# Row-wise reciprocal sums by a 32 by 32 turn and a trip through DRAM, packed remainder products, and a new order

## The chip, the cores and the metric

The kernel runs as one program on one core of a Trainium2 chip. The metric is device microseconds of one execution. The engines are TensorE (PE in the rows; its weight loads are PEld), VectorE (DVE), ScalarE (ACT), GpSimd (POOL) and SyncE (SP), which here only issues transfers.

## The reference

Three stages follow each other: attention with a threshold, a Fourier mixer with a channel MLP, and a token mixer with a gate.

```python
# 1. attention, B=4, H=8, S=576, D=64
scores = (q @ k.T) / sqrt(64)
scores = where(scores >= max(scores) - tau, scores, -1e9)
attn = exp(scores - max(scores)); attn = attn / (sum(attn) + 1e-9)
x = concat_heads(attn @ v)                      # [4, 576, 512]
# 2. Fourier mixing, then an MLP of 512 -> 2048 -> 512
u = x + real(fft(fft(x, axis=1), axis=2))
un = (u - mean(u)) / sqrt(var(u) + 1e-6)
x = u + relu(un @ w_ch1) @ w_ch2
# 3. token mixing with a gate, then a channel layer
theta = x @ w_theta
u = x + w_tok_r @ (x * cos(theta)) + w_tok_i @ (x * sin(theta))
out = u + relu(u @ w_ch)
```

## The kernel before, in words

All work is first described as named operations of one engine each, with a cost, a priority, what it comes after and which buffers it takes. A planner (`Plan.schedule`) then simulates the engines and writes the operations out in the order that it found. A long table (`SHIFT`) adds numbers to the priorities of single operations. On the chip every engine runs its own list strictly in that order and waits at semaphores.

**Attention.** The 32 heads go in 16 pairs (`pair`, p = 0 to 15). A pair has nine score tiles of 128 rows by 576 columns. For one tile TensorE makes the scores (`S`, lines 454 to 470), VectorE takes the negated row maximum (`evac`, line 478), ScalarE the exponential (`exp`, line 483), VectorE or GpSimd the bound (`bound`, lines 487 and 489), VectorE the masked product with the row sum in the same instruction (`mask`, line 494), TensorE transposes the result (`turn`, lines 501 and 541) and ScalarE copies it out of PSUM (`hi`, lines 510, 548, 550). When nine tiles are done, TensorE multiplies with the values into two banks `O` (`pv`, line 571, 256 and 320 columns), and VectorE multiplies each with the reciprocal sums into `xT` (`mu` and `mul`, line 576). The banks `O` are four; transposes, Fourier products and the reciprocal rows take theirs from the same four.

**The reciprocal sums.** The sums of a pair are nine columns of a [128, 9] tile, one per score tile: a sum sits in the partition of its row. The product at line 576 needs them along the free dimension, repeated over 64 partitions for each head. `norm_ops` does that: GpSimd adds 1e-9 (line 596), VectorE takes the reciprocal (599), GpSimd spreads eight columns to 512 (`Re`, 604), TensorE transposes four blocks (`Rt` part 0, line 611) and one more for the fifth column (part 1, line 613), and ScalarE copies both out of PSUM (`Rc`, lines 620 and 624).

**Fourier part.** `fft(b)` handles one of four batches, four pairs each. GpSimd and VectorE fold the tokens and channels, so that real transforms of quarter length are left, for an even and an odd kind. A few channels are left over: SyncE copies them into 16 rows of `exs` (line 721), ScalarE writes their rounded high part to `eys` (742) and GpSimd the low part into `exs` (746). The first transform is six products per kind and stage (`Xm`, line 775) and two more with `eys` and `exs` (`X`, line 785). The token rows beyond 128 of a kind go to `xrest`, high and low part in two slices, 31 or 33 rows each. The second transform (`Y`, line 814) uses three products for the main rows and three for `xrest`.

**Afterwards.** The channel MLP (lines 1102 to 1251; products at 1194 and 1214 to 1216) and the token mixer (1351 to 1551) are long runs of TensorE products. The MLP's normalised rows already go a way that the change uses too: VectorE turns 32 by 32 blocks (1150), SyncE stores them to DRAM in four transfers (990) and loads them back transposed (1158), and ScalarE reads them (1161).

**Transfers.** SyncE issues nearly all of them, in one list. Per pair that is a load of queries and keys (`raw`, line 304), the values (`vr`, 418), four copies into `L` (336, 337), eight into `H` and `X` (345, 346) and two corners (352). A transfer also waits for the one that used its completion semaphore eight transfers earlier.

**The start.** TensorE runs seven pairs of products on the identity (`warm`, line 393) while the first loads are under way; six pairs stand ahead of the first scores. The first scores (line 454) need a load of keys and one piece of queries that ScalarE scales (line 399, 384 columns).

Of the kernel before, what the change touches and what calls it, by code (L numbers as in the profile page):

```python
# [9 lines left out]
F32 = mybir.dt.float32  # L10
# [10 lines left out]
HS = S // 2  # L21
# [246 lines left out]
def attention_and_fft(pl, tc, ident, tb, pss, left, middle, right, qk, vv, cfk, cst, csr, u_d):  # L268
# [17 lines left out]
    ctr = lp.tile([128, 2, 640], F32R, name="ctr")  # L286
    xrest = lp.tile([128, 2, 258], F32R, name="xrest")
# [9 lines left out]
    def load_qk(p):  # L297
# [51 lines left out]
        def corner(e):  # L349
            for h, q in ((0, 512), (1, 0)):  # L350
# [5 lines left out]
        pl.op(("raw", p), *(("ACT", 620, -16.5) if first else ("SP", 2200, prio[0])), dma, [("ks", 4)] if first else (), [raw],  # L356
              delay=4500, fixed=p < 3)
# [11 lines left out]
              delay=4000)  # L369

# [4 lines left out]
    def load_first():  # L375
# [29 lines left out]
        pl.op("first pair", None, 0, -30, begin, (), [x])  # L405
        for i in range(WARM):
            after = [("warm", i - 1)] if i else []
            pl.op(("warm", i), "PE", 900 if i < 4 else 432, -40 + i, warm, after, [("O", "warm", i)])
# [6 lines left out]
    def load_v(p):  # L415
        def dma(e):
            VR[p] = new("vr", [128, 12, 64], f"vr{p}")
            e.dma_start(VR[p][:], vv[heads(p)])

        d, s = LOADS[7]  # L420
        pl.op(("vr", p), "SP", 1400, pr(9 * p - 9 + d, s) if p else -9, dma, [] if p > 1 else [("ks", 4)],
              [("vr", p)], delay=5000, fixed=p < 2)


    def pair(p):
# [3 lines left out]
        def tile_ops(idx):  # L429
# [61 lines left out]
            def mask(e):  # L491
                if "sums" not in st:
                    st["sums"] = mp.tile([128, 9], F32, tag="sums", bufs=3, name=f"sums{p}")
# [26 lines left out]
            pl.op(("S", k), "PE", 1060 if p == 0 else mm(6 if idx == 4 else 4, HS) + 25, pr(g - 1, 2), scores,  # L520
# [6 lines left out]
            pl.op(("mask", k), "DVE", 737, pr(g + 1, 7), mask, [("exp", k), ("bound", k)], (), [ps, P])  # L527
# [32 lines left out]
        def pv_ops(half, g):  # L560
# [12 lines left out]
            def mul(e):  # L573
                if p % 4 == 0 and not half:
# [7 lines left out]
            pl.op(("pv", k), "PE", 5 * TWO_PASS * n / 256 + 250, pr(g, 3), mms, deps + [("vr", p)], [O],  # L582
                  [("vr", p), ("pt5", p, 0), ("pt5", p, 1), (f"p0{half}", p), (f"p1{half}", p)])
            after = [("pv", k), ("Rc", p, half)] + ([("mu", p)] if half else []) + ([("mul", 4 * b)] if p % 4 else [])
            made = [xT] if p % 4 == 0 and not half else []
            pl.op(("mul" if half else "mu", p), "DVE", dve(n), pr(g + 1, 7.5), mul, after, made,
                  [O, ("R", p)] + ([] if made else [xT]))

        def norm_ops(g):
# [4 lines left out]
            def guard(e):  # L594
                st["rr"] = mp.tile([128, 9], F32, tag="rr", bufs=3, name=f"rr{p}")
                e.tensor_scalar(st["rr"][:], st["sums"][:], 1e-9, None, op0=ALU.add)
# [46 lines left out]
        norm_ops(g0 + 10)  # L643
# [6 lines left out]
    def fft(b):  # L650
# [82 lines left out]
        def extra_zero(e):  # L733
            if b == 0:
                e.memset(f32(xrest.rearrange("p a b->p (a b)")), 0.0)
# [8 lines left out]
        def extra_lo(e):  # L744
            x = exs[32:48, :289]
            e.tensor_sub(x.bitcast(F32R), x, f32(eys[32:48, :289]))
# [13 lines left out]
        def rows(kind, st):  # L760
            return slice(0, 128) if st < 2 else slice(64, 97) if kind == "e" else slice(0, 31)

        def first_ops(kind, st):
            loc = {}
            q = rows(kind, st)
            m = q.stop - q.start
            ki = "eo".index(kind)
            c0 = (0, size(kind) - 128, 128)[st]
# [10 lines left out]
            def part(i):  # L779
                return xrest[q, i] if st == 2 else X[kind][i][:, st]  # L780

            def more(e):
                ps = loc["ps"]
                for x, last in ((eys, False), (exs.bitcast(F32R), True)):
                    e.matmul(ps[:m, :258], x[:, c0:c0 + m], ctr[:, ki, :258], start=False, stop=last)
# [14 lines left out]
            pl.op(("Xm", k), "PE", mm(6, 258) + 80, pr(g, 3), mms, [("fl", (b, kind, a)) for a in range(2)] + ["tables"] +  # L800
                  gate(g), [O], [(f"{t}{kind}", b) for t in ("gh", "gl")])
            pl.op(("X", k), "PE", mm(2, 258), pr(g, 3), more, [("Xm", k), ("el", b)], (), [O, ("ex", b), ("ey", b)])
            pl.op(("Xh", k), "ACT", act(258), pr(g + 1, 4.2), hi, [("X", k)] + ([("Xh", (b, kind, 0))] if st else []),
# [1204 lines left out]
```

## Time and profile before

| | |
|---|---|
| time, median of 3 runs | 962.85 us (959.27 to 965.37) |
| the profiled execution | 962.4 us, span 960.5 us |
| TensorE busy | 937.9 us (98%) |
| VectorE busy | 626.9 us (65%) |
| ScalarE busy | 441.7 us (46%) |
| GpSimd busy | 301.9 us (31%) |

The span is from the first to the last instruction; the other 1.9 us of the profiled execution lie around it. A TensorE product's end is modelled, so a row of products that waits in between looks busier than it is; the distance from start to start of products that stand back to back is what one costs. The shares are means over two different halves: attention and most of the Fourier part until about 327 us, where four engines hand small tiles to each other, and the MLP and the mixer after it.

### The profile page before, as it was taken

The numbers are of one execution on the slowest core, as the hardware profiler recorded it, in microseconds if no ns is written. First come the engines' busy times: TensorE is split into PE (matmuls) and PEld (weight loads), VectorE is DVE, ScalarE is ACT, GpSimd is POOL, SyncE is SP. The second block draws the span as 40 slices with busy tenths as digits, with TensorE's granted clock in tenths as the row PEclk, the third lists the DMA queues.
The fourth block names the chain that finished last, engine by engine and source line by source line (L and its number), as shares of the span: only waits on it lengthen the run. The fifth ranks groups of instructions, "written<-read, shape, count | busy, mean of one in ns | idle before, by whom it ended". The sixth has DMA issues, their size and how long they took to land.

```text
span 960.5 us, 15977 instructions
## 1 busy us (share of the span) xinstructions
PE 937.9 (98%) x5746; PEld 807.1 (84%) x5746; DVE 626.9 (65%) x1225; ACT 441.7 (46%) x835; POOL 301.9 (31%) x468
## 2 busy tenths in 40 slices
PE   8899999999999999999999999999999999999998
PEld 6666788788778788888888888999988899999998
DVE  6777888898898889963553255232257475486832
ACT  6777877787777645530332132011143242253500
POOL 3466656657664643520232032000000021130100
PEclk9999999999999999999999999999999999999999
DMA  6897747765772478645893575241518612213011
GB/s 180 217 218 177 192 122 189 188 187 123 230 188 63 148 221 239 193 132 127 227 291 131 118 218 187 67 86 46 164 30 302 180 41 66 53 56 91 23 51 50
DMA packets 136623, 139.53 MB, mean 145 GB/s; under 512 B 77536, under 2 KB 98720, under 8 KB 136160
## 3 DMA queue, kind: packets, MB, share of 16 engines
q1 hardware_dynamic: 135520, 134.87, 50.9%
q0 software_dynamic: 720, 2.76, 1.1%
q8 instruction: 46, 0.75, 0.3%
q10 hardware_dynamic: 304, 0.87, 0.3%
q14 instruction: 33, 0.27, 0.1%
HBM read 77.34 MB, written 32.05 MB: 114 GB/s over the span
## 4 chain that ended last, share of the span: by engine, by line
PE 80%; DVE 5%; ACT 3%; DMA 2%; issue 1%; SPq 0%; DVEq 0%; POOL 0%
PE h L1194 20%; PE y L1474 12%; PE acc L1216 7%; PE acc L1214 7%; PE acc L1215 7%; PE f L1539 5%; PE th L1351 5%; PE O L571 5%; PE T L501 3%; PE ps L469 2%; PE ps L470 2%; DVE P L494 1%; DVE c L478 1%; ACT P L483 1%; PE ps L464 1%
## 5 line engine op out<-in xcount | busy, mean ns | idle before, releaser
L1194 PE MATMUL h<-uh,w 128*128 128x512 f32 (+1 forms) x640 | 197.5, 370 | 0.1
L1199 ACT ACTIVATE hh<-h 128x512 fp32r<-128x512 f32 (+1 forms) x80 | 44.4, 555 | 222.4 <-PE acc L1215 166.3
L1203 DVE SCALAR_TENSOR_TENSOR hl<-h,hh 128x512 fp32r<-128x512 f32 (+1 forms) x80 | 50.7, 634 | 135.9 <-ACT hh L1199 135.8
L1194 PEld LDWEIGHTS h<-uh,w 128*128 128x128 f32 x640 | 118.8, 188 | 17.3 <-DVE hl L1203 0.2
L494 DVE SCALAR_TENSOR_TENSOR P<-ps,c,P 128x576 f32<-128x576 f32 x144 | 115.1, 813 | 11.7 <-ACT P L483 9.2
L478 DVE TENSOR_REDUCE c<-ps 128x1 f32<-128x576 f32 x144 | 106.1, 750 | 21.1 <-PE ps L470 13.4
L1194 PE MATMUL h<-ul,w 128*128 128x512 f32 (+1 forms) x320 | 118.1, 369 | 0.0
L483 ACT ACTIVATE P<-ps,c 128x576 f32<-128x576 f32 x144 | 105.9, 749 | 22.5 <-DVE c L478 19.1
L1214 PE MATMUL acc<-w,hh 128*128 128x512 f32 x288 | 112.8, 392 | 0.0
L1216 PE MATMUL acc<-w,hl 128*128 128x512 f32 x288 | 112.6, 391 | 0.0
L1215 PE MATMUL acc<-w,hh 128*128 128x512 f32 x288 | 112.4, 390 | 0.0
L1474 PE MATMUL y<-w,z 128*128 128x288 f32 x768 | 106.9, 294 | 0.0
L1474 PEld LDWEIGHTS y<-w,z 128*128 128x128 f32 x768 | 104.0, 188 | 0.9
L501 PE MATMUL T<-ident,P 128*128 128x128 f32 x576 | 83.7, 275 | 4.6 <-DVE P L494 2.0
L510 ACT COPY pt<-T 128x512 f32<-128x512 f32 (+1 forms) x160 | 83.8, 555 | 9.1 <-PE T L501 8.2
L571 PE MATMUL O<-pt,vr 128*64 128x256 f32 (+1 forms) x640 | 84.7, 411 | 0.5 <-ACT R L624 0.5
L469 PE MATMUL ps<-H,L 128*128 128x288 f32 x240 | 75.7, 332 | 3.7 <-DVE P L494 3.0
L501 PEld LDWEIGHTS T<-ident,P 128*128 128x128 f32 x576 | 66.7, 140 | 11.7 <-ACT pt L510 4.5
L571 PEld LDWEIGHTS O<-pt,vr 128*64 128x64 f32 x640 | 43.1, 137 | 31.2 <-issue 3.9
L1194 PEld LDWEIGHTS h<-ul,w 128*128 128x128 f32 x320 | 60.1, 188 | 8.9
L470 PE MATMUL ps<-X,L 128*128 128x288 f32 x240 | 67.0, 295 | 0.0
L1216 PEld LDWEIGHTS acc<-w,hl 128*128 128x128 f32 x288 | 54.1, 188 | 11.8
(358 smaller groups left out, 1678.5 us busy)
## 6 DMA issues: line engine op xcount, KB each, us to landing
raw<-in_qk SPq DMA_DIRECT2D x14, 608.0 KB
vr<-in_vv SPq DMA_DIRECT2D x16, 384.0 KB
w<-w_d SPq DMA_DIRECT2D x6, 992.0 KB
H<-hs SPq DMA_DIRECT2D x30, 160.0 KB
X<-raw SPq DMA_DIRECT2D x30, 160.0 KB
X<-hs SPq DMA_DIRECT2D x30, 160.0 KB
H<-raw SPq DMA_DIRECT2D x30, 160.0 KB
mu<-u_d SPq DMA_DIRECT2D x18, 256.0 KB
```

The lines of the kernel that those rows point to most:

```text
L469: e.matmul(ps[:, half, :HS], L[:, qo:qo + 128], H[:, ko:ko + HS], start=(j == 0), stop=False)
L470: e.matmul(ps[:, half, :HS], L[:, qo:qo + 128], X[:, ko:ko + HS], start=False, stop=(j == n - 1))
L478: e.tensor_reduce(loc["c4"][:, 0:1], loc["ps"][:, :, :HS], axis=AXES.XY, op=ALU.max, negate=True)
L483: e.activation(halves(), loc["ps"][:, :, :HS], AF.Exp, bias=loc["c4"][:, 0:1], scale=1.0)
L494: e.scalar_tensor_tensor(halves(), loc["ps"][:, :, :HS], loc["c4"][:, 1:2], halves(), op0=ALU.is_ge, op1=ALU.mult, accum_out=st["sums"][:, ...
L501: e.transpose(T[:, kt * 128:(kt + 1) * 128], P[:, kt * 128:(kt + 1) * 128], ident[:])
L571: e.matmul(O[64 * h:64 * h + 64, :n], w, x, start=(kt == 0), stop=(kt == 4))
L1194: e.matmul(loc["ps"][:, :n], a, x[:, c, :n], start=(k == 0), stop=(k == 11))
L1214: e.matmul(a, hh[:, q], wh, start=(f == 0), stop=False)
L1215: e.matmul(a, hh[:, q], wl, start=False, stop=False)
L1216: e.matmul(a, hl[:, q], wh, start=False, stop=(f == NF - 1))
L1474: e.matmul(loc["ps"][:, half, :HS], z[:, cs], w, start=(n == 0 and m == 0), stop=(n == 8 and m == 2))
```

## The change: what it does

For pairs 4 to 15 `turned_ops` replaces `norm_ops`. The sums stand in one of three fixed [128, 32] tiles. VectorE takes the reciprocal and turns the tile in 32 by 32 blocks, so that each sum column becomes a row of 32 numbers in each of four partition groups. SyncE stores that to DRAM as 32 rows of 128 (16 KB), and then loads from there with a repeating pattern into 64 partitions per head: 576 numbers for the first head, 64 and 512 for the second (295 KB in all). No TensorE, ScalarE or GpSimd copy is left in it. Pairs 0 to 3 keep the old way.

In the Fourier part the low parts of the left-over channels go to other rows of `eys`, so that one product does the work of the two at line 785. `xrest` becomes one slice with the high part in some rows and the low part in others, so two products do the work of three at line 814. The even kind's third stage now comes after the odd kind's. `warm` falls from seven to four. The planner's costs of SyncE's loads change, the tables of constants load later, and the table of shifts has another last part, so that the whole order is new.

```diff
+TURNED_FROM = 4
-WARM = 7
+WARM = 4
...
-    ctr = lp.tile([128, 2, 640], F32R, name="ctr")
-    xrest = lp.tile([128, 2, 258], F32R, name="xrest")
+    ctr = lp.tile([128, 2, 898], F32R, name="ctr")
+    xrest = lp.tile([128, 258], F32R, name="xrest")
...
+    sums = [mp.tile([128, 32], F32, name=f"sums{i}") for i in range(3)]
...
-            after = [("pv", k), ("Rc", p, half)] + ([("mu", p)] if half else []) + ([("mul", 4 * b)] if p % 4 else [])
+            after = [("pv", k), ("Rc", p, half) if p < TURNED_FROM else ("rl", p)] + ([("mu", p)] if half else []) + ([("mul", 4 * b)] if p % 4 else [])
...
+        def turned_ops(g):
+            loc = {}
+            def guard(e):
+                e.tensor_scalar(sums[p % 3][:, :9], sums[p % 3][:, :9], 1e-9, None, op0=ALU.add)
+            def flip(e):
+                x = sums[p % 3]
+                e.reciprocal(x[:, :9], x[:, :9])
+                loc["t"] = mp.tile([128, 32], F32, tag="rt", bufs=2, name=f"rt{p}")
+                e.transpose(loc["t"][:], x[:])
+            def put(e):
+                e.dma_start(rr_d[p][:].rearrange("t (i j)->i t j", i=4), loc["t"][:])
+            def fetch(e):
+                R = st["R"] = new("R", [128, S], f"R{p}")
+                for h, q, t, o, n in ((0, 0, 0, 0, S), (1, 512, 4, 64, 64), (1, 0, 5, 0, 512)):
+                    e.dma_start(R[64 * h:64 * h + 64, q:q + n], bcast(rr_d[p][t:t + 1, o:o + 1], n, 64))
+            R = ("R", p)
+            pl.op(("guard", p), "POOL", 165, pr(g, 8.9), guard, [("mask", (p, i)) for i in range(9)])
+            pl.op(("inv", p), "DVE", 250, pr(g, 9), flip, [("guard", p)])
+            pl.op(("rs", p), "SP", 620, pr(g, 9.05), put, [("inv", p)], delay=2500)
+            pl.op(("rl", p), "SP", 1700, pr(g, 9.1), fetch, [("rs", p)], [R], delay=2500)
...
-        norm_ops(g0 + 10)
+        (norm_ops if p < TURNED_FROM else turned_ops)(g0 + 10)
...
-                for x, last in ((eys, False), (exs.bitcast(F32R), True)):
-                    e.matmul(ps[:m, :258], x[:, c0:c0 + m], ctr[:, ki, :258], start=False, stop=last)
+                e.matmul(ps[:m, :258], eys[:, c0:c0 + m], ctr[:, ki, 640:], start=False, stop=True)
...
-                mms += [(ctr[:, w, rest * 128:rest * 128 + 128], xrest[:, i]) for w, i in ((0, 0), (1, 0), (0, 1))]
+                mms += [(ctr[:, w, rest * 128:rest * 128 + 128], xrest[:]) for w in range(2)]
...
-FPLAN = {("e", 0): 13, ("e", 1): 15.1, ("e", 2): 17.2, ("o", 0): 19.3, ("o", 1): 21.4, ("o", 2): 23.5,
+FPLAN = {("e", 0): 13, ("e", 1): 15.1, ("e", 2): 23.5, ("o", 0): 17.2, ("o", 1): 19.3, ("o", 2): 21.4,
```

TensorE's list at the end of the last pair, before (T are transposes, R the reciprocal rows, xt the tokens, O the product with the values, of which ten follow):

```order
L541 MATMUL T515_1_4814<-ident_66,P15_5_4712 128x128
L541 MATMUL T515_1_4814<-ident_66,P15_7_4689 128x128
L501 MATMUL T15_6_4820<-ident_66,P15_5_4712 128x128 x4
L501 MATMUL T15_8_4826<-ident_66,P15_7_4689 128x128 x4
L611 MATMUL R15_0_4838<-ident_66,R15_4832 128x128 x4
L825 MATMUL xt2_0_1_4845<-ident_66,xT2_2753 128x128 x4
L571 MATMUL O15_0_4851<-pt15_00_4591,vr15_4371 64x256
```

The same place now, and behind the ten products of the first bank the products of the MLP's first tile `h0_0` up to the second bank:

```order
L505 MATMUL T15_6_4718<-ident_66,P15_5_4602 128x128 x4
L852 MATMUL xt2_0_1_4728<-ident_66,xT2_2770 128x128 x4
L545 MATMUL T515_1_4736<-ident_66,P15_5_4602 128x128
L545 MATMUL T515_1_4736<-ident_66,P15_7_4577 128x128
L575 MATMUL O15_0_4744<-pt15_00_4491,vr15_4263 64x256
```

```order
L1222 MATMUL h0_0_4764<-uh0_3512,w0_4715 128x512
L1222 MATMUL h0_0_4764<-ul0_3513,w0_4715 128x512
L1222 MATMUL h0_0_4764<-uh0_3512,w0_4715 128x512 x2
L1222 MATMUL h0_0_4764<-ul0_3513,w0_4715 128x512
L1222 MATMUL h0_0_4764<-uh0_3512,w0_4715 128x512 x2
L1222 MATMUL h0_0_4764<-ul0_3513,w0_4715 128x512
L1222 MATMUL h0_0_4764<-uh0_3512,w0_4715 128x512 x2
L1222 MATMUL h0_0_4764<-ul0_3513,w0_4715 128x512
L1222 MATMUL h0_0_4764<-uh0_3512,w0_4715 128x512
L575 MATMUL O15_1_4785<-pt15_01_4493,vr15_4263 64x320
```

The R rows are gone from TensorE, and the twelve products of `h0_0`, which stood behind both banks, now stand between them.

SyncE's list after pair 5's reciprocals, where the store of the turned sums and the loads of the rows are new, with the eight copies for pair 7 between them:

```order
L606 DMA rr_d5_122<-rt5_1734 4x32x32
L345 DMA H7_1755<-hs7_1525 64x640
L346 DMA X7_1756<-raw7_1308 64x640
L345 DMA X7_1756<-hs7_1525 64x640
L346 DMA H7_1755<-raw7_1308 64x640
L345 DMA H7_1755<-hs7_1525 64x640
L346 DMA X7_1756<-raw7_1308 64x640
L345 DMA X7_1756<-hs7_1525 64x640
L346 DMA H7_1755<-raw7_1308 64x640
L611 DMA R5_1819<-rr_d5_122 64x576
L611 DMA R5_1819<-rr_d5_122 64x64
L611 DMA R5_1819<-rr_d5_122 64x512
```

The list had only the eight copies there; four transfers per pair are added, and the first load waits until the store has landed.

VectorE's list from pair 15's reciprocal to its two products, now:

```order
L601 RECIPROCAL sums0_202<-sums0_202 128x9
L603 STREAM_TRANSPOSE rt15_4726<-sums0_202 128x32
L1091 TENSOR_TENSOR w0_4715<-v('w', 0)_3768,w0_4715 128x1024
L859 TENSOR_TENSOR u2_0_1_4759<-xt2_0_1_4728,sm2_0_4644 128x256
L861 TENSOR_TENSOR u2_0_1_4759<-xt2_0_1_4728,dm2_0_4613 128x4x63
L863 TENSOR_TENSOR u2_0_1_4759<-xt2_0_1_4728,dm2_0_4613 128x4
L1066 SCALAR_TENSOR_TENSOR raw('w', 2)_4659<-raw('w', 2)_4659 128x1024
L1070 SCALAR_TENSOR_TENSOR v('w', 2)_4756<-v('w', 2)_4756,raw('w', 2)_4659 128x1024
L580 TENSOR_TENSOR xT3_4039<-O15_0_4744,R15_4779 128x256
L580 TENSOR_TENSOR xT3_4039<-O15_1_4785,R15_4779 128x320
```

Six operations stand between the turn and the first product that needs the rows, where four stood between the reciprocal and it, and the two products now follow each other directly. In the other eleven turned pairs between 10 and 21 operations stand there.

## Rows read from the trace of the kernel before

**Rows 1.** The page's head and its first part.

```profile
span 960.5 us, 15977 instructions
...
PE 937.9 (98%) x5746; PEld 807.1 (84%) x5746; DVE 626.9 (65%) x1225; ACT 441.7 (46%) x835; POOL 301.9 (31%) x468
```

**Rows 2.** Busy time by window: busy us and count per engine, clock, DMA.

```profile
8.50:327.00 318.50, 303.88 (x2309) 243.88 (x2308) 271.45 (x632) 245.95 (x507) 188.55 (x363) 1.00 0.67 175
327.00:430.00 103.00, 102.34 (x506) 85.93 (x505) 90.82 (x117) 48.40 (x64) 47.74 (x35) 1.00 0.64 192
430.00:960.50 530.50, 524.68 (x2906) 470.81 (x2904) 263.91 (x471) 144.01 (x259) 63.39 (x58) 1.00 0.41 118
```

**Rows 3.** Timeline of TensorE, 104 to 117 us: start, length, operation.

```profile
105.93 0.66 PE L611 MATMUL R<-ident,R 128*128 128x128 f32 x4
106.34 0.38 PE L469 MATMUL ps<-H,L 128*128 128x288 f32 x1
...
107.49 0.27 PE L613 MATMUL R<-ident,rr 128*128 128x128 f32 x1
107.69 2.91 PE L571 MATMUL O<-pt,vr 128*64 128x320 f32 x20
...
113.44 0.37 PE L785 MATMUL Xe<-ctr,eys 128*128 128x258 f32 x1
113.65 0.29 PE L785 MATMUL Xe<-ctr,exs 128*128 128x258 f32 x1
113.77 0.60 PE L501 MATMUL T<-ident,P 128*128 128x128 f32 x4
```

**Rows 4.** Waits, 8.5 to 327 us: total us, times, longest.

```profile
DVE c L478 <- PE ps L470: 13.4, 19, 5.2
...
ACT R L624 <- PE R L613: 11.2, 8, 4.1
...
DVE P L494 <- ACT P L483: 9.2, 22, 2.3
...
ACT R L620 <- PE R L611: 7.1, 7, 2.1
...
DVE xT L576 <- PE O L571: 5.7, 6, 1.6
```

**Rows 5.** VectorE's groups, 8.5 to 327 us: busy, mean ns, idle before.

```profile
L494 DVE SCALAR_TENSOR_TENSOR P<-ps,c,P 128x576 f32<-128x576 f32 x144 | 115.1, 813 | 11.7 <-ACT P L483 9.2 <-POOL rr L596 0.3 <-POOL R L604 0.3
L478 DVE TENSOR_REDUCE c<-ps 128x1 f32<-128x576 f32 x144 | 106.1, 750 | 21.1 <-PE ps L470 13.4 <-PE ps L454 5.0 <-PE ps L464 2.1
...
L599 DVE RECIPROCAL rr<-rr 128x9 f32<-128x9 f32 x16 | 3.3, 206 | 1.1 <-POOL rr L596 1.1
```

**Rows 6.** ScalarE's copies of the reciprocal rows, whole span.

```profile
L620 ACT COPY R<-R 128x512 f32<-128x512 f32 x16 | 9.3, 584 | 7.4 <-PE R L611 7.1
...
L624 ACT COPY R<-R 64x64 f32<-64x64 f32 x32 | 6.6, 206 | 11.5 <-PE R L613 11.2
```

**Rows 7.** Timeline of SyncE, 629 to 651 us: the MLP's trip through DRAM.

```profile
630.50 1.94 SPq L990 DMA_DIRECT2D un_d<-un  x4
...
633.99 0.38 SPq L1158 DMA_DIRECT2D ul<-un_d  x1
```

**Rows 8.** Timeline of ScalarE, same stretch: the reader of those rows.

```profile
637.11 0.62 ACT L1161 CAST uh<-ul 128x512 fp32r<-128x512 f32 x1 [1.37 <-DMA ul<-un_d]
```

**Rows 9.** Timeline of SyncE, 158 to 170 us: one of eight copies.

```profile
164.87 0.60 SPq L345 DMA_DIRECT2D H<-hs  x1
```

**Rows 10.** Timeline of the start, all engines.

```profile
1.46 5.20 PEld L393 LDWEIGHTS warm<-ident 128*128 128x128 f32 x24 [1.46 <-POOL ident masks.py:199]
...
4.41 0.62 ACT L399 ACTIVATE x<-x,tb 64x384 f32<-64x384 f32 x1 [1.60 <-DMA x<-in_qk]
...
6.88 3.49 PE L454 MATMUL ps<-x 64*128 64x288 f32 x12
...
10.30 0.52 PEld L393 LDWEIGHTS warm<-ident 128*128 128x128 f32 x4 [0.39 <-issue]
```

More of the change, by code (lines that the diff above doesn't have):

```diff
@@ L265, in heads, with attention_and_fft @@
     return p + 3 - 2 * (p % 4)
-def attention_and_fft(pl, tc, ident, tb, pss, left, middle, right, qk, vv, cfk, cst, csr, u_d):
+def attention_and_fft(pl, tc, ident, tb, pss, left, middle, right, qk, vv, cfk, cst, csr, u_d, rr_d):
     nc = tc.nc
@@ L369, in load_qk @@
               delay=4000)
+    sums = [mp.tile([128, 32], F32, name=f"sums{i}") for i in range(3)]
+    for i in range(3):
+        pl.op(("sz", i), "POOL", 100, -25 + i, lambda e, i=i: e.memset(sums[i][:], 0.0))
     corners = [rp.tile([128, 128], F32R, name=f"corner{i}") for i in range(2)]
@@ L758, in gate, with rows @@
             return [("S", divmod(int(g), 9))] if b < B - 1 and g < 9 * NP else []
-        def rows(kind, st):
-            return slice(0, 128) if st < 2 else slice(64, 97) if kind == "e" else slice(0, 31)
+        def rows(kind, i):
+            return slice(64 * i, 64 * i + 33) if kind == "e" else slice(64 * i + 32, 64 * i + 64)
         def first_ops(kind, st):
             loc = {}
-            q = rows(kind, st)
-            m = q.stop - q.start
             ki = "eo".index(kind)
-            c0 = (0, size(kind) - 128, 128)[st]
+            m = 128 if st < 2 else (33, 32)[ki]
+            c0 = (0, size(kind) - 128, 128 - ki)[st]
             def mms(e):
@@ L799, in first_ops @@
             g = g0 + fp[kind, st]
-            pl.op(("Xm", k), "PE", mm(6, 258) + 80, pr(g, 3), mms, [("fl", (b, kind, a)) for a in range(2)] + ["tables"] +
+            pl.op(("Xm", k), "PE", mm(6, 258) + 80, pr(g, 3), mms, [("fl", (b, kind, a)) for a in range(2)] + ["tables", ("el", b)] + ([("Y", (b - 1, 1), kind)] if b else []) + [("X", (b, "o", 2))] * (st == 2 and not ki) +
                   gate(g), [O], [(f"{t}{kind}", b) for t in ("gh", "gl")])
-            pl.op(("X", k), "PE", mm(2, 258), pr(g, 3), more, [("Xm", k), ("el", b)], (), [O, ("ex", b), ("ey", b)])
-            pl.op(("Xh", k), "ACT", act(258), pr(g + 1, 4.2), hi, [("X", k)] + ([("Xh", (b, kind, 0))] if st else []),
+            pl.op(("X", k), "PE", mm(1, 258), pr(g, 3), more, [("Xm", k), ("el", b)], (), [O, ("ey", b)])
+            pl.op(("Xh", k), "ACT", act(258), pr(g + 1, 4.2), hi, [("X", k)] + ([("Xh", (b, kind, 0))] if st else []) + ([("Xl", (b, "o", 2))] if st == 2 and not ki else []),
                   [] if st else xs, [O] + (xs[:1] if st else []))
@@ L1823 @@
[L1823 to L1826 removed]
[6 rows of a table removed]
[17 rows of a table added]
+    (('Yp',), -36.02), (('a2',), 18.17), (('bound',), 18.79), (('bound', 0, 3), 123.45), (('bound', 12, 8), -65.39),
@@ L1863, in body @@
         x3_d = [dram.tile([128, 512], F32, name=f"x3_d{i}") for i in range(NT)]
+        rr_d = [dram.tile([32, 128], F32, name=f"rr_d{i}") for i in range(NP)]
         un_d = [dram.tile([512, 128], F32, name=f"un_d{i}") for i in range(NT)]
@@ L1938, in tables @@
     csr = np.zeros((128, 640))
-    for ki, r0, first in ((0, 64, (0, 0)), (1, 0, (1, 1))):
+    for ki, r0, first in ((0, 0, (0, 0)), (1, 33, (1, 1))):
         for par in range(2):
```

111 lines of the change are left out of this document (53 added, 58 removed), and 115 rows, old and new, of the table SHIFT.

## The prediction

> **What bounds the kernel now.** I read the page's head first: TensorE is busy 937.9 of 960.5 us [rows 1]. The view by window then shows that this is two cases [rows 2]. From 327 us on TensorE hardly rests (102.34 of 103 us, then 524.68 of 530.5), so there a product more or less counts with its full length. From 8.5 to 327 us the page still says 303.88 of 318.5, but ends of products are modelled, VectorE is busy 271.45 (85%) and ScalarE 245.95 (77%), and the list of waits has each waiting for another: VectorE 13.4 us for scores, 9.2 for exponentials, 5.7 for the products with the values [rows 4]. I take that stage as a pipeline of small tiles with TensorE as the densest engine and VectorE close behind. What is taken from TensorE there comes back in part.
>
> **What TensorE loses.** The cost of a product that does not wait is its distance to the next start [rows 3]. Four R transposes take 0.41 us (105.93 to 106.34), the lone one 0.20 (107.49 to 107.69): 0.61 a pair, times twelve pairs 7.3 us. A left-over product takes 0.12 us (113.65 to 113.77) and up to 0.21 with a change of tile before it (113.44 to 113.65). 24 go at line 785 (24 groups, one each) and 20 at line 814 (five groups in each of four batches, one each): 44 × 0.12 = 5.3 us, at most 9.2; the next products follow without a change, so I take 5.3. By the new order 31 of the 44 stand before the last pair's products and 13 behind. So TensorE loses 7.3 + 3.7 = 11.0 us in the stage and 1.6 behind it. The 1.6 counts whole. Of the 11.0 I count half, 5.5: nothing of it if VectorE sets the pace, all if TensorE does, and the rows put the two at 85% and at most 95%.
>
> **What ScalarE and GpSimd lose.** Per turned pair ScalarE loses a copy of 0.584 us and two of 0.206, 12.0 us in all [rows 6], and it no longer stands still in front of them (11.2 and 7.1 us for all sixteen pairs) [rows 4]. ScalarE at 77% hides that, except where an exponential was late; the 9.2 us of VectorE's waiting are the most there is. I count it inside the half above. GpSimd's spreading copy goes too; GpSimd has the most slack of the four [rows 2], so nothing.
>
> **What VectorE gains.** Twelve turns of 128 by 32. The trace has none of that size; the reciprocal of nine columns before it takes 0.206 us [rows 5], and a 576-column maximum 0.75. A turn lies nearest to the reciprocal: 0.2 × 12 = 2.4 us, bounds 0 and 9. VectorE has idle time of 15% next to it; half on the path, 1.2 us.
>
> **The new wait.** The product with the reciprocal rows stands in VectorE's strict list, so rows that come late stop VectorE and, behind it, every score tile. The same way through DRAM exists in the MLP: the last of four stores starts about 1.94 × 3/4 after 630.50, so near 631.95; the load that waits for it is issued at 633.99, 2.0 us later, and its reader, which waited for nothing else, starts at 637.11, 3.1 us after the issue [rows 7, 8]. The change's loads are three: the last starts about 0.9 us behind the first at 0.38 to 0.60 each [rows 7, 9]. With an idle list the way is 2.0 + 0.9 + 3.1 = 6.0 us.
>
> What VectorE has to do meanwhile follows from the new order and from durations. After pair 4's turn come four maxima at 0.75, four masked products at 0.81 and two small ones at about 0.21: 6.7 us of work, and at VectorE's 85% some 7.8 us of time. The same count gives 7.8 us for pair 10, 9.0 to 9.1 for 5, 8 and 14, 9.7 for 11, and 11.3 to 14.7 for 6, 7, 9, 12 and 13. Pair 15 has six operations of 3,580 columns together, at 0.813 us per 576 columns an estimate of 5.0 us, 5.9 in time. So eleven pairs have room for 6.0 us. Pair 5's loads stand behind eight copies of 0.6 us [rows 9]: 0.5 + 4.8 + 0.9 + 3.1 = 9.3 us, late by 0.3. Pair 15 has two weight loads of 512 KB between its store and its loads; at the stage's 175 GB/s [rows 2] these alone move for 6.0 us, so its rows are up to 5 us late. TensorE has `h0_0` and a bank of values for that time, of 2.75 and 2.8 us (twelve products of 512 columns, and ten of 320), so I count nothing for it, and nothing for the earlier `h0_0`. Lateness: 0.3 us.
>
> The four added transfers on SyncE take 4 × 0.6 = 2.4 us a pair, of about 20. Their neighbours wait 2 us more when a load stands directly behind its store, as for pairs 4 and 9. The loads for the next pairs are issued nearly a pair ahead, which hides that; without this cover each would cost its 2 us, 4 in all. That is in the range, not in the sum. The larger constant table and its later loads lie beside this work as well.
>
> The Trainium skill speaks against this step: "VectorE: DVE Perf Modes", section "Rules for kernel authors", sends a 128 by 128 transpose to TensorE, because VectorE turns only 32 by 32 blocks. The rows agree that TensorE's own price is small, 0.61 us a pair, and that the trip through DRAM is ten times as long; by that rule the exchange would lose, which is the rival "late rows" below. By the sum it does not, since the trip occupies neither engine.
>
> **The start.** 24 weight loads of `warm` take 5.20 us and the first scores start at 6.88, though the first piece that ScalarE scales was ready at 5.03 [rows 10]. Sixteen end near 5.0. That frees up to 1.7 us; since the next steps are VectorE's, I take 0.7.
>
> **Sum.** -5.5 - 1.6 - 0.7 + 1.2 + 0.3 = -6.3 us. The profiled execution took 962.4 us, 1.9 more than its span, and gives 956.1; the median of the runs is 0.45 us higher. I forecast **956.5 us**, 0.7% below 962.85. About 1% is what a measurement of this kernel can tell from no change: 953.2 and 972.5 us are its bounds.
>
> **The rivals.**
> - Half the relief arrives, as above: 956.5, own range 951 to 961. Chance 0.44.
> - *TensorE sets the pace of the stage.* For it: its busy share is the highest there. Against: it waits for VectorE and ScalarE too. Then 11.0 + 1.6 + 1.7 go, and the turn costs nothing: 962.85 - 14.3 = 948.5. Chance 0.24.
> - *VectorE sets it.* For it: 85% busy, with maxima and masked products that nothing shortens. Against: 28 us of waiting for TensorE and ScalarE. Only 1.6 + 0.7 go and the turns cost 2.4: 962.4, no gain. Chance 0.17.
> - *Late rows.* The trip through DRAM ends behind the bulk copies on the same queue in most pairs. For it: the queue's engines are 67% busy in the stage [rows 2], and only one trip in the trace is clean enough to read. Against: the 3.1 us above are for 256 KB, nearly the same bytes. With a trip of 11.5 us pairs 4 and 10 are late by 3.7 each, 5, 8 and 14 by 2.5, 11 by 1.8: 16.7 us, against 6.6 us of gains, 973: slower than before. It decides at a trip of about 9.8 us. Chance 0.10.
> - *A cold start.* In the trace the first 24 weight loads come 0.217 us apart and the four at 10.30 come 0.13 apart [rows 10]: the granted clock rose from its lower level (1.2 GHz) to 2.4 GHz in between, after TensorE had worked on `warm` without a break. With a third of that gone it may rise later. Pair 0's nine score groups at half the clock take about 1.9 us instead of 1.0, against 1.6 of VectorE's work, so some 3 us over nine: 959.5. Chance 0.05. The Trainium skill, "TensorE: Matmul & The Clock Gate", Part 1, says that throttled is the default and sustained activity releases it; the trace agrees in direction, and no run here has a shorter `warm`.
>
> That the change does not do what it says is excluded by the order: the R rows are gone in twelve pairs.
>
> **Range and chances.** 946 to 966 leaves out the lower edge of the second case and the late rows' upper half, under 2 in 10. Faster by over 1%: nearly all of the second case and a quarter of the first, 0.35. Slower by over 1%: over half of the late rows, 0.06. Within 1%: 0.59.
>
> **What would show it.** The last product of pair 15 with its rows (line 576; the end of the first long window, 327 us, was put there) moves to about 321 if the half is right, 315 if TensorE set the pace, and stays if VectorE did. VectorE's waits at line 580 for transfers of R: under 2 us without pair 15 if the trip is 6 to 8 us; over 10 if late rows decide. Twelve turns near 0.2 us. First scores near 5.2 us, and at the second clock level by about 8 us. From there to the end TensorE's busy share stays near 99%; new holes in the MLP, where the order is also new, would make the forecast too low.

## The result: 973.4 us, slower by 1.2%

The changed kernel takes 973.39 us (median of 4 runs, 972.58 to 976.79), the kernel before 962.0 beside it: ratio 1.0123, interval [1.0082, 1.0165]. The forecast was 956.5 us, range 946 to 966. The profiled execution is the longest of the four, 976.79 us with a span of 975.0.

The page's first part, and the windows cut where the last product of pair 15 ends (342.4 us now, 327 before), as in [rows 1, 2]:

```profile
span 975.0 us, 15763 instructions
...
PE 938.3 (96%) x5630; PEld 800.6 (82%) x5630; DVE 618.3 (63%) x1236; ACT 433.7 (44%) x805; POOL 286.6 (29%) x454
```

```profile
8.50:342.40 333.90, 305.83 (x2221) 239.55 (x2220) 271.76 (x637) 238.48 (x475) 178.37 (x352) 0.99 0.68 178
342.40:445.00 102.60, 98.96 (x474) 81.85 (x473) 84.94 (x115) 45.23 (x61) 49.02 (x30) 0.98 0.62 190
445.00:975.00 530.00, 526.60 (x2918) 473.35 (x2916) 260.07 (x478) 146.58 (x264) 57.03 (x57) 1.00 0.41 119
```

In a row of windows stand its bounds and length, then busy us and count of TensorE, its weight loads, VectorE, ScalarE and GpSimd, then the granted clock, the DMA share and GB/s. The first window has become 15.4 us longer; from its end to the span's end it is 632.6 us against 633.5. The whole loss lies in the attention stage. TensorE has 88 products fewer there and yet 28.1 us without work in place of 14.6. The waits of the stage (8 to 345 us), against [rows 4]:

```profile
ACT P L488 <- DVE c L483: 33.1, 31, 3.7
ACT pt L514 <- PE T L505: 20.8, 26, 2.7
DVE c L483 <- PE ps L475: 11.8, 25, 1.8
DVE P L498 <- ACT P L488: 11.4, 22, 2.1
...
DVE xT L580 <- DMA R<-rr_d: 10.5, 8, 3.9
DVE c L483 <- PE ps L459: 8.6, 8, 3.5
...
DVE u L859 <- DMA u_d<-u: 5.5, 2, 4.3
...
DVE bs L1135 <- DMA mu<-u_d: 2.3, 2, 1.9
```

and all of VectorE's waits for transfers before, in the same window:

```profile
DVE u_t L832 <- DMA u_d<-u: 2.2, 2, 1.9
...
DVE u L832 <- DMA u_d<-u: 1.8, 1, 1.8
```

VectorE's waits for transfers have grown from 4.0 to 18.3 us: those for the rows (line 580, 10.5 us) and for loads of `mu` (2.3) are new, and the wait for the store that frees the one buffer of `u` now has a stop of 4.3 us where the longest was 1.9. The other engines then wait for VectorE. Pair 5 shows the first, in the timelines of SyncE, VectorE and TensorE:

```profile
123.37 0.58 SPq L606 DMA_DIRECT2D rr_d<-rt  x1
124.05 0.48 SPq L345 DMA_DIRECT2D H<-hs  x1
...
129.35 0.59 SPq L346 DMA_DIRECT2D H<-raw  x1
129.99 2.00 SPq L611 DMA_DIRECT2D R<-rr_d  x3
```

```profile
130.89 0.76 DVE L483 TENSOR_REDUCE c<-ps 128x1 f32<-128x576 f32 x1 [1.17 <-PE ps L469]
135.53 0.42 DVE L580 TENSOR_TENSOR xT<-O,R 128x256 f32<-128x256 f32 x1 [3.88 <-DMA R<-rr_d]
```

```profile
131.44 1.15 PE L505 MATMUL T<-ident,P 128*128 128x128 f32 x8
136.01 0.66 PE L505 MATMUL T<-ident,P 128*128 128x128 f32 x4 [3.42 <-DVE xT L580]
```

The turn had ended at 122.1. The store, eight copies and three loads stand one behind the other; the rows are used 13.4 us after the turn, VectorE stands 3.88 us and TensorE 3.42. What follows has a price of its own: the granted clock falls to its lower level (1.2 GHz) for 3.4 us behind this stop of TensorE and behind that of 3.56 us for `u`, which ends at 259 us, as the windows show (mean clock third from the end). By an estimate, half of 3.4 us, each fall costs at most 1.7 us. A third, at 358.6 us, lies behind the stage.

```profile
136.70:140.10 3.40, 3.40 (x17) 3.38 (x16) 2.76 (x7) 2.73 (x6) 2.45 (x4) 0.50 0.27 96
259.60:263.00 3.40, 3.40 (x15) 1.60 (x16) 3.17 (x9) 2.43 (x4) 3.19 (x4) 0.50 0.74 206
```

### The profile page after: what moved, and what is told of

Its sections match the earlier page's. It is cut to its first block, busy times and chain, and to the rows that moved or that the text cites. A ratio compares the mean times of both kernels' runs of the same rounds, so it can differ in the third digit from the quotient of the medians.

```text
span 975.0 us, 15763 instructions
## 1 busy us (share of the span) xinstructions
PE 938.3 (96%) x5630; PEld 800.6 (82%) x5630; DVE 618.3 (63%) x1236; ACT 433.7 (44%) x805; POOL 286.6 (29%) x454
## 4 chain that ended last, share of the span: by engine, by line
PE 73%; DMA 9%; DVE 7%; ACT 4%; SPq 3%; issue 2%; POOL 1%; DVEq 0%; ACTq 0%; POOLq 0%
PE h L1222 20%; PE y L1502 12%; PE acc L1242 7%; PE acc L1244 7%; PE acc L1243 7%; PE f L1567 5%; PE th L1379 5%; PE O L575 3%; DVE c L483 2%; DMA R<-rr_d 2%; PE T L505 2%; DMA H<-hs 2%; DVE P L498 2%; PE ps L459 2%; ACT P L488 2%
## 5 line engine op out<-in xcount | busy, mean ns | idle before, releaser
L498 DVE SCALAR_TENSOR_TENSOR P<-ps,c,P 128x576 f32<-128x576 f32 x144 | 114.9, 813 | 13.5 <-ACT P L488 11.4
L505 PE MATMUL T<-ident,P 128*128 128x128 f32 x576 | 86.6, 280 | 14.7 <-DVE xT L580 4.3
L1411 POOL TENSOR_TENSOR tok<-tok 128x512 f32<-128x512 f32 x8 | 10.6, 1321 | 223.8 <-ACT tok L1401 123.0
```

Source lines behind the costliest of these rows:

```text
L498: e.scalar_tensor_tensor(halves(), loc["ps"][:, :, :HS], loc["c4"][:, 1:2], halves(), op0=ALU.is_ge, op1=ALU.mult, accum_out=st["sums"][:, ...
L505: e.transpose(T[:, kt * 128:(kt + 1) * 128], P[:, kt * 128:(kt + 1) * 128], ident[:])
```

## The experiments

Theory A: the transfers of the rows cost the time, since the rows come late. A2: not by their own lateness, but by what they do to the other transfers in SP's list. B: the cold start costs it. C: the new order of the work. Later A2w (SP's wait for the store), D (bytes on the DMA engines), L (SP's issue time) and P (packets) divide A2. "Ratio" is always to the kernel before on the same chip.

**Twelve identity products ahead of the scores, as before.**

```diff
-            for i in range(2):
...
+            warmed.append(0)
+            for i in range(6 if len(warmed) == WARM else 2):
```

> The changed kernel with four more products of the identity ahead of the first scores, 12 instead of 8, as the kernel before has; nothing else differs. Theory A (the rows of the sums come late and TensorE waits): the cold start is a small matter, its 4.7 us at the end of pair 0 have shrunk to 1.5 us by pair 2, so the time stays within 1.5 us of 973.4 us. Theory B (the cold start carries through): the full clock is granted near 8 us instead of 20.7 us, and the time falls by 4 to 5 us, to about 969 us.

Measured: 973.05 us, 1.014 [1.0112, 1.0169]. Of B's 4 to 5 us nothing shows, and the fastest of the four runs is 971.74: B falls. A gain or loss of a microsecond could not be told here.

**Rows not read, and no transfers at all.** The first edit; the second run also leaves out the store and the loads.

```diff
-                e.tensor_mul(xTs[b][:, j, a:a + n], loc["O"][:, :n], st["R"][:, a:a + n])
+                R = f32(cfs[:]).rearrange("p a b c d->p (a b c d)") if p >= TURNED_FROM else st["R"]
+                e.tensor_mul(xTs[b][:, j, a:a + n], loc["O"][:, :n], R[:, a:a + n])
```

> The changed kernel in which the products of pairs 4 to 15 with the reciprocal rows read a constant table in SBUF in place of the rows (the output is then not normalised for these pairs). The turns, the store and the three loads of every pair are still issued, and nobody waits for them. Theory A, in its direct form (VectorE's wait for the rows is the loss): the 10.5 us of waits at line 580 go, and the half-clock stretch behind the longest of them, so 961 to 965 us. Theory A2 (the loss is SP's list: four more issues per pair make SP's other transfers late): little goes, 968 to 973 us. Theory C (the new order of the work on the engines loses by itself): 970 us or more, and the next run shows no gain either.

> As the run whose products read a constant table, and the store and the three loads of each of the pairs 4 to 15 are not issued at all (the output of these pairs is not normalised); TensorE's relief and VectorE's turns stay. Theory A and theory A2: 956 to 961 us, since the transfers cause all of the loss but the cold start. They differ in how much of it the run before this one had already. Theory C: 970 us or more. My own prediction of 956.5 us assumed the transfers to cost 0.3 us, so this run also prices the relief without them: 956 us with half of it on the path, 950 us with all of it.

Measured: 968.86 us, 1.009 [1.0063, 1.0118], and 958.32 us, 0.9978 [0.9959, 0.9997]. Reading the rows costs some 4.5 us (973.4 - 968.9; the two ratios' intervals overlap, but each of the eight runs with readers, of the changed kernel and of the one with twelve products, is slower than each of the four without); having the transfers at all, read by nobody, 10.5 (968.9 - 958.3). Theory A in its direct form is the smaller part, A2 the larger, C is not needed for the loss.

**The short warm-up in the kernel before.** Two of its identity groups emit nothing.

```diff
...
+            warmed.append(0)
+            if len(warmed) in (5, 6):
+                return
```

> The kernel before with only 8 of its 12 products of the identity ahead of the first scores, all else as it was. Theory B (what starts cold stays late): full clock near 20 us, and 4 to 5 us more, 966 to 967 us. Theory A (the late start is made up within a few pairs, because VectorE or ScalarE sets the pace there): within 1.5 us of 962 us.

Measured: 961.95 us, 1.0027 [0.9999, 1.0056]. That is 2.6 us more [-0.1, 5.4]. The last masked product comes 5.0 us late in pair 0 and 2.7 in pair 15 of its profile. Between the two expectations, and small.

**The same transfers from other queues:** from ScalarE, from GpSimd (`nc.gpsimd`), and the loads alone from ScalarE.

```diff
-                e.dma_start(rr_d[p][:].rearrange("t (i j)->i t j", i=4), loc["t"][:])
+                nc.scalar.dma_start(rr_d[p][:].rearrange("t (i j)->i t j", i=4), loc["t"][:])
...
-                    e.dma_start(R[64 * h:64 * h + 64, q:q + n], bcast(rr_d[p][t:t + 1, o:o + 1], n, 64))
+                    nc.scalar.dma_start(R[64 * h:64 * h + 64, q:q + n], bcast(rr_d[p][t:t + 1, o:o + 1], n, 64))
```

> The changed kernel with the store and the three loads of the rows issued by ScalarE instead of SP, at the same places of the program. The run without the transfers took 958.3 us, the one in which they run unread 968.9 us. Theory A2 (what costs is their place in SP's list: the four issues and the wait for the store hold back SP's other transfers): SP's list is as without them, so 960 to 966 us, what is above 958 being ScalarE's own price for four issues and one wait per pair. Theory D (their bytes hold up the 16 DMA engines): no gain, 969 us or more.

> As the run with ScalarE, but GpSimd issues the store and the three loads. Theory A2: 960 to 966 us; GpSimd is busy 287 us of 975, less than ScalarE with 434 us, so not above the run with ScalarE. Theory D: 969 us or more.

> The changed kernel with the store of the rows on SP and only the three loads on ScalarE: SP is rid of three issues and of the wait for the store, ScalarE takes them. Theory A2w: SP's other transfers are on time, 965 to 970 us, what is above 958 being the rows' own lateness (4.5 us) and ScalarE's issues and waits. Theory D: 972 us or more.

Measured: 971.73 us, 1.0135 [1.0098, 1.0172]; 984.85 us, 1.026 [1.0229, 1.0291]; 983.84 us, 1.0233 [1.0206, 1.0261]. All three miss A2's numbers, but don't speak for D either: the issuing engine now stands still itself. From ScalarE, VectorE's waits for exponentials are 20.7 us (11.4 in the changed kernel) and the waits for the rows still 9.6. Those for the store of `u` are 1.8 us there (5.5 in the changed kernel) and none for `mu` is left, so SP's list is relieved as A2 has it, and the time is paid elsewhere. GpSimd stands 14.9 us for the store, with its small steps for VectorE behind it:

```profile
DVE P L498 <- ACT P L488: 20.7, 33, 2.0
DVE xT L580 <- DMA R<-rr_d: 9.6, 6, 5.1
...
DVE u L859 <- DMA u_d<-u: 1.8, 2, 1.2
```

```profile
POOL R L611 <- DMA rr_d<-rt: 14.9, 6, 4.7
```

**Sixteen bytes per transfer,** with the products reading the constant table; in the second run the loads read what the store wrote.

```diff
-                e.dma_start(rr_d[p][:].rearrange("t (i j)->i t j", i=4), loc["t"][:])
+                e.dma_start(rr_d[p][:1, :4], loc["t"][:1, :4])
...
-                    e.dma_start(R[64 * h:64 * h + 64, q:q + n], bcast(rr_d[p][t:t + 1, o:o + 1], n, 64))
+                    e.dma_start(R[64 * h:64 * h + 1, q:q + 4], bcast(cst[0:1, 0:1], 4, 1))
```

> As the run whose products read a constant table (pairs 4 to 15 are not normalised), SP still issues one store and three loads per pair, but each moves 16 bytes, and the loads take them from a constant in DRAM and so don't wait for the store. What is left of the transfers is four issues, some 2.4 us of SP's list per pair. Theory A2 by the issues: near the 968.9 us of the run with the full transfers unread, 965 to 969 us. Theory A2 by the wait for the store, or theory D (bytes): near the 958.3 us without transfers, 958 to 961 us.

> As the run with 16 bytes per transfer, but the three loads read what the store has just written, so that SP waits for it (pairs 4 to 15 are not normalised). The mirror of the run before: theory A2w: 967 to 969 us; theory D: 960 to 963 us.

Measured: 960.69 us, 1.0004 [0.9982, 1.0025], and 959.57 us, 0.9998 [0.9982, 1.0014]. Waiting for the store costs nothing that shows. So 8 us depend on what the transfers carry.

**Two loads in place of three,** with a source that walks over the two halves, then 64 repeats, then the columns.

```diff
-                for h, q, t, o, n in ((0, 0, 0, 0, S), (1, 512, 4, 64, 64), (1, 0, 5, 0, 512)):
-                    e.dma_start(R[64 * h:64 * h + 64, q:q + n], bcast(rr_d[p][t:t + 1, o:o + 1], n, 64))
+                for q, o, step, n in ((0, 0, 640, 512), (512, 512, 64, 64)):
+                    x = rr_d[p][:1, :1]
+                    src = bass.AP(tensor=x.tensor, offset=x.offset + o, ap=[[step, 2], [0, 64], [1, n]])
+                    e.dma_start(R[:, q:q + n], src)
```

> The changed kernel with two loads of the rows per pair instead of three, which move the same bytes: one for the first 512 queries of both halves, one for the other 64 of both. Theory A2 by the issues: one of the four issues goes, 0.6 us per pair, so about a quarter of the 10.5 us that the unread transfers cost, 970 to 971.5 us. Theory A2 by the wait for the store, or theory D: as the changed kernel, 973 us.

Measured: 1020.14 us, 1.0651 [1.0596, 1.0706], which no theory had. Waits of VectorE and, behind it, of TensorE's weight loads, 8 to 400 us:

```profile
DVE xT L580 <- DMA R<-rr_d: 56.0, 20, 5.9
PEld T L505 <- DVE xT L580: 28.0, 11, 5.6
```

The loads land later (more on this in the last section). It is a large dose of lateness: 56.0 - 10.5 = 45.5 us more of waiting at line 580, 3.8 us a pair, and 46.7 us more time. TensorE's weight loads stand 28.0 us of it with VectorE, and its clock has fallen often: the mean granted clock is 0.91 here between 100 and 400 us (third from the end), and 0.99 in the changed kernel between 100 and 345 us.

```profile
100.00:400.00 300.00, 249.08 (x1720) 202.32 (x1720) 211.30 (x495) 175.00 (x346) 132.47 (x265) 0.91 0.57 143
```

So the near equality of 45.5 and 46.7 is not a price of one for one: in the changed kernel, taking away 10.5 us of the same waiting gave back 4.5.

**Bytes, packets or SP's time.** Four variants with the rows unread, the full store, and the loads from a constant: with all bytes; with half the columns; with 64 different rows in place of one row 64 times; with 16 bytes in each of the 64 packets. The fifth is the kernel with 16-byte transfers of one packet, with seven loads instead of three.

```diff
...
+                    e.dma_start(R[64 * h:64 * h + 64, q:q + n], bcast(csr[0:1, 0:1], n, 64))
...
+                    e.dma_start(R[64 * h:64 * h + 64, q:q + n // 2], bcast(csr[0:1, 0:1], n // 2, 64))
...
+                    e.dma_start(R[64 * h:64 * h + 64, q:q + n], csr[64 * h:64 * h + 64, 0, :n])
...
+                    e.dma_start(R[64 * h:64 * h + 64, q:q + 4], bcast(csr[0:1, 0:1], 4, 64))
...
+                    for k in range(3 if q else 2):
+                        e.dma_start(R[64 * h + k:64 * h + k + 1, q:q + 4], bcast(cst[0:1, 0:1], 4, 1))
```

> As the run whose products read a constant table (pairs 4 to 15 are not normalised) with the full transfers, but the three loads of each pair take as many bytes from a constant in DRAM, and so don't wait for the store. Four issues with 16 bytes each took 960.7 us, with their full bytes and the wait for the store 968.9 us: 8.2 us lie between. Theory A2w (SP stands at the first load until the store has landed, and all behind it in its list is late): without the wait 960 to 963 us. Theory D (the bytes hold up the DMA engines): 967 to 969 us.

> As the run with the loads from a constant (969.4 us; pairs 4 to 15 are not normalised), but each of the three loads takes half as many columns: as many packets, half the bytes, 144 KB per pair in place of 288 KB. If the volume is what costs, half of the 9 us over the runs with 16 bytes goes, 964 to 966 us. If the number of packets costs (64 for each load), 968 to 970 us. If the loss sets in only above some volume, about 960 us.

> As the run with the loads from a constant, with the same bytes in the same packets, but each of the 64 partitions reads a row of its own from DRAM, in place of all 64 reading the same row. If it is the repeated reading of one row that is slow, 960 to 964 us; if it is the volume on the DMA engines, 968 to 971 us.

> As the run with the loads from a constant (pairs 4 to 15 are not normalised), but each of the 64 packets of a load carries 16 bytes. The records show that SP takes 0.62 to 0.66 us to issue a load of 64 packets, with full or half bytes, and 0.30 us for one of a single packet, so that the 48 transfers of the runs with 16 bytes took 15 us of SP's list and those of the others 30 us. Theory L (SP's time is what costs): as with the full bytes, 967 to 969 us (against a kernel before at 960 to 961). Theory D (bytes): 960 to 962 us.

> As the run with 16 bytes per transfer in one packet (pairs 4 to 15 are not normalised), with seven loads per pair in place of three: 8 issues of 0.30 to 0.37 us, again some 30 us of SP's list over the stage, with next to no bytes and packets. Theory L: 966 to 969 us. Theory P (the number of packets on the DMA engines costs, not SP's time): 960 to 962 us.

Measured, with SP's issue records of the rows between 90 and 330 us added up (48 records, 96 in the third row; 44 of 48 are in the trace of the last), and VectorE's waits for `u` and `mu` between 8 and 345 us in the one profiled execution:

| rows' transfers per pair | SP, us | waits, us | median us | ratio |
|---|---|---|---|---|
| none | 0 | 3.2 | 958.32 | 0.9978 [0.9959, 0.9997] |
| 4 of one packet, 16 bytes | 15.3 | 6.3 | 960.69 | 1.0004 [0.9982, 1.0025] |
| 8 of one packet, 16 bytes | 26.7 | 7.8 | 963.63 | 1.0029 [1.0016, 1.0041] |
| loads of 64 packets, 16 bytes each | 29.3 | 9.0 | 965.18 | 1.0067 [1.0043, 1.0092] |
| half the bytes | 30.1 | 8.2 | 968.49 | 1.0058 [1.0035, 1.0081] |
| all bytes, 64 different rows | 29.5 | 10.8 | 967.51 | 1.0039 [1.0015, 1.0063] |
| all bytes, constant, no wait | 31.1 | 9.5 | 969.40 | 1.0086 [1.0057, 1.0116] |
| all bytes, waiting for the store | 30.5 | 10.2 | 968.86 | 1.0090 [1.0063, 1.0118] |
| as changed, and read | 27.7 | 7.8, and 10.5 for the rows | 973.39 | 1.0123 [1.0082, 1.0165] |

The expectation of 966 to 969 us for eight short issues was missed. By the ratios four short transfers cost 2.5 us over none, and eight 2.4 over four; each of these steps is within the noise, the two together are not. The 64 packets cost more than the eight short issues by a hair (their intervals miss each other by 0.0002, at 29.3 and 26.7 us of SP's time), with next to no bytes in them. So transfers cost time by their place in SP's list, without bytes, and by this narrow margin more with many packets; whether by the packets themselves, or because a load of 64 holds SP 0.6 us at a time and a short one 0.3, no run separates. From there to all bytes the intervals overlap: half the bytes met the number for packets, 64 different rows neither of theirs, and whether the volume, or reading one row 64 times, adds anything is not settled. SP's own waits for earlier transfers don't explain the loss: between 90 and 330 us they add up to 6.0 us without the transfers, 7.6 with all bytes from a constant and 12.4 with the eight short ones. My first step to theory D, from the runs with 16 bytes, was wrong: these had cut packets and SP's time along with the bytes.

Where it comes out is the same in these traces: in VectorE's waits of the third column. By the ends of the second products with the rows, the kernel with the rows unread is 1.0 us behind the one without transfers at pair 8, 5.4 at pair 9, where VectorE waits 2.9 us for `mu` and the clock then falls, 7.6 at pair 11, where it waits for `u`, and 8.9 at pair 15. VectorE's timeline without transfers, then with all bytes from a constant:

```profile
234.86 0.15 DVE L862 TENSOR_TENSOR u<-xt,sm 128x4 f32<-128x4 f32 x1
...
241.73 0.43 DVE L858 TENSOR_TENSOR u<-xt,sm 128x256 f32<-128x256 f32 x1 [1.87 <-DMA u_d<-u]
```

```profile
198.83 0.69 DVE L1136 BATCH_NORM_STATS2 bs<-mu 128x6 f32<-128x512 f32 x1 [2.89 <-DMA mu<-u_d]
...
241.12 0.15 DVE L864 TENSOR_TENSOR u<-xt,sm 128x4 f32<-128x4 f32 x1
...
250.75 0.42 DVE L860 TENSOR_TENSOR u<-xt,sm 128x256 f32<-128x256 f32 x1 [4.63 <-DMA u_d<-u]
```

and SP's, of that store, in the same two kernels:

```profile
237.56 0.71 SPq L902 DMA_DIRECT2D u_d<-u  x1
```

```profile
245.01 0.33 SPq L904 DMA_DIRECT2D u_d<-u  x1
```

`u` is ready at 235.0 and 241.3, its store is issued 2.6 and 3.7 us later, behind the rest of eight copies, and the next `u` starts 4.2 and 5.7 us after the issue. Both legs have grown: SP's list and the way behind it. These are single executions; the times above carry the verdict. In the run without transfers VectorE waits for no load of `mu` there.

**The relief alone, in the order of before.** Pairs 4 to 15 have neither spreading copy, transposes nor row copies, and read the table.

```diff
...
+                    if p >= 4:
+                        pass
-                    if part == 0:
+                    elif part == 0:
                         for t in range(4):
                             e.transpose(T[:, t * 128:(t + 1) * 128], st["R"][:, t * 128:(t + 1) * 128], ident[:])
...
```

> The kernel before, in its own order, in which pairs 4 to 15 have no rows at all: neither GpSimd's spreading, nor TensorE's five transposes, nor ScalarE's three copies, and the products read a constant table (these pairs are not normalised). It prices TensorE's relief without any transfer and without the new order. By my prediction, half of 11.0 us and all of 1.6 us: 7 us less than before, about 953 us. If TensorE sets the pace throughout: 948 us. If VectorE's chain sets it: 960 us. The changed kernel without its transfers came to 958.3 us; if that is all the relief is worth, this one does too, and if it comes to 953 us the new order loses the rest.

Measured: 955.77 us, 0.9948 [0.9932, 0.9964], 5.0 us less. The 11.0 us in my expectation held the left-over products too, which this run keeps; the rows alone are 7.3 us of TensorE, half of it 3.7. Between half and all.

**A second buffer for `u` in the kernel before.**

```diff
-        return side.tile(shape, dt, tag=tag, bufs=pl.bufs[tag], name=name)
+        return side.tile(shape, dt, tag=tag, bufs=pl.bufs[tag] + (tag == "u"), name=name)
```

> The kernel before, in its own order, with a second buffer for the tile u whose store VectorE waits for. In its trace VectorE stands 1.8 us at u and 2.2 us at u_t, 4.0 us in four places, where it waits for the store of the tile before. If these waits are on the path that sets the pace, as the longer ones in the changed kernel seem to be, 956 to 958 us against 960 to 961; if TensorE has work ready meanwhile, no change. (In the changed kernel there is no room in SBUF for a second one.)

Measured: 959.22 us, 0.9978 [0.9958, 0.9999]: 2.1 us less, and no wait for that store is left in the stage. It is the one complete kernel here ahead of the kernel before, by little. In the changed kernel the effect of a second buffer was not tried, so what `u` alone costs there is open.

## Why the prediction was wrong

In place of gains of 6.6 us and a lateness of 0.3, the runs give gains of 2.1, 10.5 for the transfers and 4.5 for reading what they bring: 12.9 us more, against 11.4 [7.9, 15.9] measured.

**The four added transfers on SyncE: the step that failed.** I counted them as hidden, 4 us at most, and put nothing into the sum. They cost 10.5 us with nobody reading them. I had costed SP's time (2.4 us a pair, right: 0.6 us each for the store and a load) and looked for who is behind them among the loads issued a pair ahead. Behind them also stand transfers that are needed within a few us: the store that frees `u`, the loads of `mu`, the copies of H and X. That issues are made nearly a pair ahead holds for the loads, not for these. 2.4 us in 20 is little in the mean, but not behind a run of eight copies.

**Lateness 0.3 us: the second failure.** The idle-list trip of 6.0 us is not contradicted by pairs 4, 10 and 14, whose products came 7.4 to 7.8 us after the turn without waiting; that bounds the trip and does not measure it. Where the product waited, in eight pairs, it came 9.5 to 13.4 us after the turn. Pair 5 was to be late by 0.3 and was by 3.9: the store left 1.2 us after the turn, the copies took 5.9 us instead of 4.8, the issue of the three loads 2.0. For pair 15, to which I gave nothing, VectorE waited 2.8 us, but TensorE, with the bank of values and four transposes to do, stood only 0.9. Reading the rows costs 4.5 us of time.

**The rival "late rows", 973 us, met the number with part of the mechanism and some luck.** In the eight pairs that waited, the product came 11.5 us after the turn in the mean, which is the trip that the rival took. But it had pairs 4, 10 and 14 late, which were not, and 16.7 us of lateness where VectorE waited 10.5 (7.7 without pair 15, between the two signs of the prediction). Taking the readers away gives back only about a third of the loss; the rest is the transfers behind, of which the rival has nothing. The rule of the Trainium skill that I weighed against the change ("VectorE: DVE Perf Modes", "Rules for kernel authors") would have led to the right sign here; the price of the exchange showed in the transfers, which that section does not speak of.

**TensorE's relief:** 5.0 us for the rows in the order of before, with the copies of ScalarE and GpSimd that go with them, where half of TensorE's 7.3 is 3.7. The relief, the left-over products, the turns and the new order together came to 2.1 us [0.3, 3.9] in the run without transfers, where I had 6.6. The runs don't separate the order and the packing, so this remainder of about 3 us against the relief alone is open, and with it whether the new order costs something.

**VectorE's turns:** twelve at 211 to 214 ns, as forecast.

```profile
L603 DVE STREAM_TRANSPOSE rt<-sums x12: 211/211/214, 105.2 to 331.6; 128x32 f32<-128x32 f32 x12
```

**The start, -0.7 us:** the first scores came at 5.29 us, as forecast, but at the lower clock, granted full only from 20.7 us. The timelines of TensorE in the changed kernel and in that without transfers, which start alike, against [rows 10]:

```profile
5.29 10.38 PE L459 MATMUL ps<-x 64*128 64x288 f32 x20
```

```profile
5.03 3.17 PE L459 MATMUL ps<-x 64*128 64x288 f32 x12
```

The last masked product of pair 0 comes 4.7 us later than before, that of pair 2 1.5 us. In the times, twelve products in place of eight change nothing that four runs of each can tell, and in the order of before eight in place of twelve cost 2.6 us [-0.1, 5.4]: the 0.7 us that I took show nowhere, and the rival's 3 us are neither shown nor excluded.

**Behind the stage:** 0.9 us less, of 1.6; TensorE is busy 98.96 of 102.60 us there, 96%, where I expected 99%.

**A slip in a rival's sum:** "VectorE sets it" comes to 962.95 us by its own terms, not 962.4. It changes no conclusion.

## What to carry to other kernels

A transfer added to a queue is paid by the transfers behind it; list those that someone needs within a few us (a store that frees a single buffer above all) before calling it hidden, and look at the bursts rather than at the queue's mean load. What a wait for data costs in the strict list of the engine that feeds the others has to be measured by taking the wait away: 10.5 us of it were worth 4.5 us here. When an experiment makes a transfer small, see which of bytes, packets and issue time it has made small.

## What the runs showed of the hardware

- **A load's issue took SP longer with 64 packets than with one, and no longer with more bytes:** 0.27 to 0.30 us for a packet of 16 bytes, 0.61 to 0.66 us for 64 packets, of 16 bytes as of 2 KB (means of 36 records or more). It does not go on growing with the packets: 128 of them, in the kernel with two loads, took 0.59 us (18 records). The timelines of SP with one packet, then with 64 of half size:

```profile
101.18 0.82 SPq L612 DMA_DIRECT2D R<-in_cst  x3
```

```profile
101.49 2.12 SPq L612 DMA_DIRECT2D R<-in_csr  x3
```

The Trainium skill, "Perfetto Trace Analysis", "What \"DMA-bound\" means", reads such slices of the issuing engine as the making of descriptors, not the moving of data; these rows agree in so far as half the bytes change nothing and one packet takes less than 64.

- **With a source that begins with a dimension of two, fewer packets ran at once.** In the changed kernel the 64 packets of 2,048 bytes run 11 to 14 at a time and are through in 1.0 to 1.9 us (the six loads whose packets can be told apart); in the kernel with two loads, whose source begins with a dimension of two, 128 packets of the same size run at most 4 at a time and take 5.5 to 6.8 us (seven loads). The Trainium skill, "DMA: Bandwidth & Descriptors", "Rules for kernel authors", says that an outermost dimension below 16 confines a transfer to at most as many DMA engines. The trace agrees in direction; which engines took the packets its records don't say.
- **The same start, warm or cold.** Of the 14 profiled executions of kernels with eight identity products in the order of the change, four (the changed kernel's among them) had the lower clock until about 20 us; the others had the full clock from 7 us or earlier, and short falls later. One profile of a start is no measurement of it.
